# One written order of issue for the attention stage of a fused attention, Fourier-mix and gated-MLP kernel

## The chip, the cores and the metric

The kernel runs on one core of a Trainium2 chip. The metric is the device time of one execution in microseconds, lower is better. The engines are TensorE (PE, matmuls; PEld is its weight load), VectorE (DVE), ScalarE (ACT), GpSimd (POOL) and SyncE (SP, which issues DMAs).

## The reference, cut to what matters

```python
def reference(**kwargs):
    attn_out = _attn_ref(q, k, v, f)      # 4 batches x 8 heads, 576 tokens, 64 channels a head
    x = attn_out.transpose(0, 2, 1, 3).reshape(B, S, H * D)
    x = _moe_ref(x, w_ch1, w_ch2)         # real part of a 2-D FFT + x, norm, relu MLP 512-2048-512
    return _moe2_ref(x, w_theta, w_tok_r, w_tok_i, w_ch)

def _attn_ref(q, k, v, f):
    scores = scale * np.matmul(q, k.transpose(0, 1, 3, 2))
    cum = np.cumsum(np.log(np.clip(f, 0.0001, 1.0)), axis=-1)
    scores = np.where(causal, -1e9, scores + cum[:, :, :, None] - cum[:, :, None, :])
    attn = softmax(scores)
    return np.matmul(attn, v)
```

The change touches the issue order of the first stage alone: attention, and the FFTs of the batches that are already done.

## The kernel before

The program has three phases. `phase1` walks over the 32 heads in pairs (two heads, g = 0 and g = 1, share one 128-row result) and does the FFT of three batches and the first normalisation between the heads; `phase2` is the MLP (`ffn1`, `ffn2`); `phase3` is the token mix and the gate.

For one head, attention does this. `prep_units`: ACT rounds the raw q and k into `hi` (L222) and copies q (L224), POOL forms the rest (`hi` L226, `kl` L228). `score_units`: five tiles of query rows, i = 4 down to 0, with 576, 448, 320, 192 and 66 key columns; each is a matmul on `hi` (L247) and one on `kl` (L248) into a PSUM bank `pa` (three banks); DVE adds the mask and keeps the row minimum (L256), ACT takes the exponential into `P` (L261). `turn_units`: 15 PE transposes of `P` (L286) into four `pb` banks (three physical ones), each copied to `PT` by DVE or, the fourth, by ACT (L289). `av_units`: for a pair of heads, 14 matmuls of `v` (64 columns wide) with `PT` into the one bank `pt` (L321). Head g = 0 writes partitions 0 to 63 and head g = 1 writes 64 to 127, so the two heads' matmuls use different halves of the array. `spread` transposes the reciprocal row sums (`wide`, L300), `evac_pair` multiplies `pt` by them (L347, into `X` or `Y`), and `fft_units` has some 87 matmuls a batch (L428, L439, L451).

In the program text the 14 matmuls alternate between the heads: for each key block and column range `for g in (1, 0)` issues both. A dependency added by hand (the loop over `copies`, with reason "one run") lets the first of the 14 go only after all eight `PT` copies of the two heads are placed.

What order the engines see is not the text's. The Tile framework's scheduler reorders `phase1` by a timeline of its own and by priorities (`high_priority(20)` for scores, `high_priority(100)` for the 14 matmuls); the opening (heads 0 and 1's preparation and head 0's scores) and everything after the sixth column of the MLP are in `manual_schedule`, where program order is kept. PSUM slots are given out in the scheduler's order.

Of the kernel before, what the change touches and what calls it, by code (L numbers as in the profile page):

```python
# [17 lines left out]
B, H, S, D = 4, 8, 576, 64  # L18
# [35 lines left out]
G = 4  # L54


def f(ap):
    return ap.bitcast(F32)


class Net:
# [37 lines left out]
    def p1_open(self):  # L99
# [22 lines left out]
        )  # L122
        h0 = self.w3.tile([128, 1600], F32R, tag="PT", name="h0", bufs=4)[64:66]
        flag = f(h0[:, 2 * S : 2 * S + 1])
        self.P = [self.w3.tile([128, 1856], F32, name=f"P{k}", bufs=1) for k in range(2)]
        ch = self.c1.tile([32, 2, S], F32R, tag="E", name="ch", bufs=2)
# [14 lines left out]
        for z in self.q2:  # L141
            nc.gpsimd.memset(f(z[64:66]), 1.0)
# [5 lines left out]
        for z in (self.xh, self.xl):  # L148
            nc.gpsimd.memset(f(z), 0.0)
# [123 lines left out]
    def turn_units(self, hd):  # L273
        nc = self.nc
        P = hd["P"]
        PT = self.w3.tile([128, 1600], F32, tag="PT", name="PT", bufs=4)
        hd["PT"], hd["copies"] = PT, []
        for bank, pieces in enumerate(TURNED):
            ps = self.bank_b()
            for j, a, b, off in pieces:  # L280
                for i in range(5):
                    if not a <= TOP[i] < b:
                        continue
                    o, n = off + TOP[i] - a, END[i] - TOP[i]
                    src = P[0:n, POFF[i] + KEY[j] : POFF[i] + KEY[j] + 128]
                    nc.tensor.transpose(ps[:, o : o + n], src, self.ident[0:n, 0:n])  # L286
            d, w = TSKIP[bank], TWIDE[bank]
            dst = PT[:, PTOFF[bank] : PTOFF[bank] + w]
            copy = nc.scalar.copy(dst, ps[:, d : d + w]) if bank > 2 else nc.vector.tensor_copy(dst, ps[:, d : d + w])  # L289
            hd["copies"].append(copy)  # L290
            yield

    def spread(self, p, T, wide):
# [10 lines left out]
    def av_units(self, m, hds, T, wide, done):  # L304
        nc = self.nc
        v = hds[0]["pair"]["v"]
        place = {
            (j, max(a, 128 * j)): PTOFF[bank] + off - TSKIP[bank] + max(a, 128 * j) - a
            for bank, pieces in enumerate(TURNED)
            for j, a, b, off in pieces  # L310
        }
        yield
        first = True
        with self.tc.high_priority(100):
            for j in range(5):
                for lo_q, hi_q in ((0, SPLIT), (SPLIT, 576)):
                    a = max(lo_q, 128 * j)
                    if a >= hi_q:
                        continue
                    for g in (1, 0):  # L320
                        ins = nc.tensor.matmul(  # L321
                            T[64 * g : 64 * g + 64, T0 + a : T0 + hi_q],
                            v[:, j, g, :],
                            hds[g]["PT"][:, place[j, a] : place[j, a] + hi_q - a],
                            start=j == 0,
                            stop=j == 4 or (j == 1 and hi_q == SPLIT),
                        )
                        if first:
                            for copy in hds[0]["copies"] + hds[1]["copies"]:
                                self.tc.add_manual_dep(  # L330
                                    ins.ins, copy.ins.name,
                                    mybir.DependencyInfo(mybir.DependencyClass.NoSync, mybir.DependencyReason.DATA),
                                    reason="one run",
                                )
                            first = False
        for _ in range(5):
            yield
        R = self.spread(m % NP, T, wide)
        yield
        done(m, T, R)  # L340
# [137 lines left out]
    def phase1(self):  # L478
        pair, heads = self.p1_open()
        NH = B * H  # L480
        pairs, heads, raws = {0: pair}, dict(enumerate(heads)), {}
        fft = None
        self.tick = 0
        rows, norm, av = iter(()), iter(()), iter(())

        def pull():
            nonlocal fft
            next(rows, 0)
            self.tick += 1
            if self.tick % 3 == 0:  # L490
                next(norm, 0)
            if (self.tick % 5 or n > 24) and fft is not None and next(fft, 0) == 0:
                fft = None

        def done(m, T, R):
            nonlocal rows, fft
            for _ in rows:
                pass
            rows = self.evac_pair(m % NP, R, T, m == B * NP - 1)
            next(rows, 0)  # L500
            if m % NP == NP - 1:
                fft = self.fft_units(m // NP, *self.EO, rows)

        for n in range(-1, NH + 1):
            a = self.score_units(heads[n + 1], (n + 1) % 2) if 0 < n + 1 < NH else iter(())
            prep = iter(())
            if n + 2 < NH:
                p, g = divmod(n + 2, 2)
                if n == 0:
                    pairs[1] = self.load_pair(1)  # L510
                if n >= 0:
                    heads[n + 2] = dict(pair=pairs[p], g=n + 2)
                    prep = self.prep_units(n + 2, pairs[p], raws.pop(n + 2), heads[n + 2])
                if n > 0 and g == 1 and p + 1 < B * NP:
                    pairs[p + 1] = self.load_pair(p + 1)
            if n + 3 < NH:
                raws[n + 3] = self.load_head(n + 3)
            m, odd = divmod(n - 2, 2)
            if m >= 0 and not odd:
                T = self.bank_t()  # L520
                av = self.av_units(m, [heads[2 * m], heads[2 * m + 1]], T, pairs[m]["rz"], done)
            t = self.turn_units(heads[n]) if 0 <= n < NH else iter(())
            if n == NH - 1:
                self.p1a.close()
                self.p2_open()
                self.load(0)
                self.load(1)
            k = n - 2
            if 0 <= k < 4:
                for j in range(2):  # L530
                    self.load_dft(2 * k + j, f(heads[n]["hi"][0:1, 0, 0:2]))
            if n == NH - 3:
                while fft is not None:
                    pull()
                t1 = self.c1.tile([128, 2, CH], F32, tag="E", name="uc1", bufs=2)
                t2 = self.c1.tile([128, 2, CH], F32, tag="O", name="uc2", bufs=2)
                t3 = self.c1.tile([128, 2, CH], F32, tag="yh", name="s12", bufs=1)
                t4 = self.c1.tile([128, 2, CH], F32, tag="yl", name="sq", bufs=1)
                t5 = self.c1.tile([128, 4], F32, tag="zh", name="rs", bufs=1)
                norm = self.norm_units(0, ((t1, t2), t3[:, 0], t3[:, 1], t4, t5))  # L540
            live = True
            while live:
                live = False
                for g_ in (t, av, a):
                    if next(g_, 0) is None and (g_ is not av or n >= NH - 1):
                        live = True
                next(prep, 0)
                pull()
                if n >= NH - 1:
                    self.fill(2)  # L550
            for _ in prep:
                pass
        for _ in norm:
            pass
        self.p1b.close()
        for _ in rows:
            pass
        self.pt.close()
        self.pso = self.ctx.enter_context(self.tc.tile_pool(name="pso", bufs=2, space=PSUM))
        return fft  # L560
# [538 lines left out]
        self.pu0.close()  # L1099


def body(tc, ins, out):
    with ExitStack() as ctx:
        net = Net(ctx, tc, ins, out)
        fft = net.phase1()
        net.phase2(fft)
        net.phase3()
# [101 lines left out]
```

## Time and profile before

| | |
|---|---|
| median of 3 runs | 940.19 us (938.8 to 942.03) |
| profiled execution, own time | 940.95 us |
| its span | 939.2 us, 15860 instructions |
| busy over the span | PE 894.1 us (95%), PEld 841.5 us, DVE 606.7 us, ACT 417.8 us, POOL 326.3 us |
| mean granted PE clock | 0.985 |

Attention takes the first 245 us or so; head 31's transposes, the last batch's FFT and the first norms reach to about 305 us; from there the MLP and the token mix fill the rest. In the trace a matmul's record lasts beyond the start of the next (the engine is pipelined), so what PE needs for a matmul is read from the distance between two starts, not from a record's length.

### The profile page before, as it was taken

How to read it: one execution, taken by the hardware profiler on the slowest of the kernel's cores; microseconds unless marked ns; L12 is line 12 of the kernel's file. 1: busy time of each engine (PE TensorE's matmuls, PEld its weight loads, DVE VectorE, ACT ScalarE, POOL GpSimd, SP SyncE). 2: the span in 40 equal slices, each digit the busy share in tenths (PEclk: the TensorE clock that was granted, in tenths of full speed). 3: DMA queues.
4: the chain of work that ended last, by engine and by line, in shares of the span. 5: the costliest groups of instructions: out<-in, count | busy, mean ns of one | idle time of the engine just before them, and what ended most of it. 6: DMA issues, size and time to landing. Idle time of an engine off the chain costs nothing.

```text
span 939.2 us, 15860 instructions
## 1 busy us (share of the span) xinstructions
PE 894.1 (95%) x5960; PEld 841.5 (90%) x5960; DVE 606.7 (65%) x1495; ACT 417.8 (44%) x1014; POOL 326.3 (35%) x369
## 2 busy tenths in 40 slices
PE   4998999989788999999999999999999999999998
PEld 3777878777577999999999999999999999999998
DVE  8676676674899943456654565536687756747563
ACT  6888678685544332222221232223235534434331
POOL 6676788676601343000000000000035635425330
PEclk9999999999979999999999999999999999999999
DMA  5643423231233300013322122514310000010001
GB/s 167 202 149 106 130 93 114 83 105 40 82 97 93 90 1 1 1 46 90 91 91 90 45 90 74 199 29 127 109 51 2 1 26 27 14 40 1 26 27 51
DMA packets 23725, 68.04 MB, mean 72 GB/s; under 512 B 2906, under 2 KB 6362, under 8 KB 23648
## 3 DMA queue, kind: packets, MB, share of 16 engines
q1 hardware_dynamic: 20608, 62.88, 21.2%
q0 software_dynamic: 2320, 2.97, 1.2%
q10 hardware_dynamic: 720, 1.18, 0.4%
q8 instruction: 47, 0.77, 0.3%
q14 instruction: 30, 0.25, 0.1%
HBM read 57.91 MB, written 9.07 MB: 71 GB/s over the span
## 4 chain that ended last, share of the span: by engine, by line
PE 62%; DVE 5%; ACT 1%; issue 1%; DMA 0%; POOL 0%; DVEq 0%; SPq 0%; ACTq 0%
PE pa L767 19%; PE pb L781 11%; PE po L781 8%; PE pb L988 7%; PE pa L999 5%; PE pa L952 5%; PE po L988 5%; PE pa L948 1%; DVE u L789 1%; DVE kra L959 1%; DVE a L587 0%; DVE a L585 0%; DVE uc L754 0%; DVE kra L962 0%; PE pb L952 0%
## 5 line engine op out<-in xcount | busy, mean ns | idle before, releaser
L767 PE MATMUL pa<-un,wf 128*128 128x384 f32 x1152 | 221.4, 342 | 6.3 <-ACT un L755 3.4
L767 PEld LDWEIGHTS pa<-un,wf 128*128 128x128 f32 x1152 | 204.6, 191 | 10.2 <-DVE un L756 4.5
L773 DVE SCALAR_TENSOR_TENSOR h<-pa,h 128x384 fp32r<-128x384 f32 x96 | 52.4, 555 | 139.0 <-ACT h L772 139.0
L781 PE MATMUL pb<-h,wf 128*128 128x384 f32 x660 | 134.2, 337 | 0.3 <-DVE u L789 0.3
L781 PEld LDWEIGHTS pb<-h,wf 128*128 128x128 f32 x660 | 116.0, 188 | 1.1 <-DVE u L789 0.6
L781 PE MATMUL po<-h,wf 128*128 128x384 f32 x492 | 105.2, 340 | 0.4 <-ACT h L772 0.2
L772 ACT ACTIVATE h<-pa 128x384 fp32r<-128x384 f32 x96 | 45.7, 489 | 132.7 <-PE pa L767 130.0
L261 ACT ACTIVATE P<-P,mn 128x448 f32<-128x448 f32 (+4 forms) x160 | 89.0, 558 | 33.6 <-DVE mn L256 33.4
L988 PE MATMUL pb<-wtk,z 128*128 128x288 f32 x513 | 98.3, 295 | 1.3 <-ACT z L977 1.3
L944 POOL COPY xd<-u 128x64 f32<-128x64 f32 x32 | 6.9, 255 | 264.5 <-DVE u L789 254.5
L256 DVE CUSTOM_DVE_ANT_0 P<-pa,mask 128x448 f32<-128x448 f32 (+3 forms) x160 | 69.4, 457 | 42.1 <-PE pa L248 35.6
L781 PEld LDWEIGHTS po<-h,wf 128*128 128x128 f32 x492 | 86.2, 188 | 3.6 <-ACT h L772 1.9
L978 POOL TENSOR_TENSOR z<-kra,z 128x256 fp32r<-128x256 f32 x72 | 53.1, 752 | 93.5 <-ACT z L977 93.4
L247 PE MATMUL pa<-hi 128*128 128x448 f32 (+1 forms) x192 | 65.8, 364 | 20.5 <-DVE hi L226 9.4
L988 PEld LDWEIGHTS pb<-wtk,z 128*128 128x128 f32 x513 | 79.3, 188 | 2.0 <-ACT z L977 2.0
L988 PE MATMUL po<-wtk,z 128*128 128x288 f32 x351 | 75.2, 295 | 0.8 <-ACT z L977 0.8
L286 PE MATMUL pb<-ident,P 128*128 128x128 f32 (+2 forms) x480 | 73.9, 284 | 1.7 <-DVE uc L724 0.9
L247 PEld LDWEIGHTS pa<-hi 128*128 128x128 f32 x192 | 38.2, 204 | 30.1 <-issue 14.5
L289 DVE COPY PT<-pb 128x448 f32<-128x448 f32 (+1 forms) x96 | 55.6, 594 | 14.2 <-PE pb L286 13.3
L952 PE MATMUL pa<-wf,xs 128*128 128x256 f32 x456 | 64.1, 289 | 0.0
L286 PEld LDWEIGHTS pb<-ident,P 128*128 128x128 f32 (+2 forms) x480 | 56.6, 147 | 7.5 <-ACT P L261 1.2
L248 PE MATMUL pa<-kl,q 66*128 66x448 f32 (+1 forms) x192 | 58.0, 337 | 1.4 <-POOL kl L228 0.7
(206 smaller groups left out, 1667.0 us busy)
## 6 DMA issues: line engine op xcount, KB each, us to landing
raw<-in_qk SPq DMA_DIRECT2D x31, 576.0 KB
raw<-in_wf SPq DMA_DIRECT2D x32, 512.0 KB
raw<-in_wtk SPq DMA_DIRECT2D x18, 288.0 KB
v<-in_vp SPq DMA_DIRECT2D x16, 320.0 KB
out<-ob SPq DMA_DIRECT2D x12, 288.0 KB
dft<-in_dft POOLq DMA_DIRECT2D x8, 346.0 KB, 5.4
raw<-in_wth SPq DMA_DIRECT2D x4, 512.0 KB
st_wth<-raw SPq DMA_DIRECT2D x4, 512.0 KB
```

The costliest lines, as they stand in the source:

```text
L247: nc.tensor.matmul(t[:, 0 : b - a], hi[:, 1, q], hi[:, 0, a:b], start=True, stop=False)
L248: nc.tensor.matmul(t[:, 0 : b - a], q2[:, q], kl[:, g, a:b], start=False, stop=True)
L256: nc.vector.tensor_tensor_reduce(out=p[:, a:b], in0=t[:, 0 : b - a], in1=self.mask[:, m0 + a : m0 + b], scale=-0.125, scalar=least, op0=AL ...
L261: nc.scalar.activation(p, p, AF.Exp, bias=lowest, scale=-1.0, accum_out=zs[:, g, i : i + 1])
L286: nc.tensor.transpose(ps[:, o : o + n], src, self.ident[0:n, 0:n])
L289: copy = nc.scalar.copy(dst, ps[:, d : d + w]) if bank > 2 else nc.vector.tensor_copy(dst, ps[:, d : d + w])
L767: nc.tensor.matmul(ps[:, 0:CH], t[:, l, 128 * d : 128 * d + 128], un[r][:, d], start=n == 0, stop=n == 11)
L773: nc.vector.scalar_tensor_tensor(h[:, 1], ps[:, 0:CH], 0.0, f(h[:, 0]), ALU.max, ALU.subtract)
L781: nc.tensor.matmul(outs[d], t[:, l, 128 * d : 128 * d + 128], h[:, r], start=k % G == 0 and n == 0, stop=k % G == G - 1 and n == 2,)
L952: nc.tensor.matmul(th, xs[:, l, d], self.wth[d][:, r, 256 * hf : 256 * hf + 256], start=n == 0, stop=n == 11)
L978: nc.gpsimd.tensor_tensor(z[:, 1], t, f(z[:, 0]), ALU.subtract)
L988: nc.tensor.matmul(acc[k][th], z[:, l, 128 * k : 128 * k + 128], self.wtk[kt][:, r, 288 * th : 288 * th + 288], start=first and i == 0 and ...
```

## The change

All calls of `phase1` on engines and queues, from the start of its loop (head 0's transposes, head 1's scores) to the point where head 31's transposes are about to be created, go to a `Recorder` instead of the builder. Then `rec.emit(order(0, n))` issues the recorded calls inside `manual_schedule` for all engines, in one fixed permutation that is written out as a string: each character gives the distance of the next call in the list of those left. So each engine keeps its part of one order, and PSUM slots follow that order. The hand-made dependency on the `PT` copies is gone, so that each of the 14 `av` matmuls has a place of its own. Which instructions there are, and their sizes, does not change. The recording ends before the last head's transposes, the last `av` run, the last FFT and the MLP; these go through the scheduler as before.

```diff
+class Recorder:
+    def __getattr__(self, name):
+        return Queue(self, name)
+
+    def emit(self, order):
+        for k in order:
+            engine, name, a, kw = self.calls[k]
+            getattr(getattr(self.nc, engine), name)(*a, **kw)
+        self.live = False
...
-            copy = nc.scalar.copy(dst, ps[:, d : d + w]) if bank > 2 else nc.vector.tensor_copy(dst, ps[:, d : d + w])
-            hd["copies"].append(copy)
+            (nc.scalar.copy if bank > 2 else nc.vector.tensor_copy)(dst, ps[:, d : d + w])
...
-                        if first:
-                            for copy in hds[0]["copies"] + hds[1]["copies"]:
-                                self.tc.add_manual_dep(
...
-                                    reason="one run",
...
+        rec = self.nc = Recorder(self.nc)
...
             if n == NH - 1:
+                with self.tc.manual_schedule():
+                    rec.emit(order(0, len(rec.calls)))
+                self.nc = rec.nc
                 self.p1a.close()
...
+DIGITS = "#$%&()*+,-./0123456789:;<=>?@ABCDEFGHIJKLMNOPQRSTUVWXYZ[]^_`abcdefghijklmnopqrstuvwxyz|"
+ORDERS = (
+    (
+        "&~$6~+X~,e~,e~,e~,e#*35=)129*+1(%((-%.*..vw#$+##///~$-#.$,(#&))#~$%$6#((<^>/#u,8B$.U%....2.~*p2#~*n5"
...
+def order(part, n):
+    left, taken, digits = list(range(n)), [], iter(ORDERS[part])
+    for c in digits:
+        k = DIGITS.find(c)
...
+        taken.append(left.pop(k))
+    return taken
```

In the rows below `pt` is the result bank of a pair of heads, `PT` the transposed probabilities (one number for each head), `P0` and `P1` the probabilities of the even and the odd head; all recorded calls carry line 71 in the changed kernel.

PE in the first pair of heads, before: the first 14 matmuls of the pair come in two runs, the heads in turn.

```order
L321 MATMUL pt_342<-PT_281,v_119 64x192
L321 MATMUL pt_342<-PT_212,v_119 64x192
L321 MATMUL pt_342<-PT_281,v_119 64x384
L321 MATMUL pt_342<-PT_212,v_119 64x384
L321 MATMUL pt_342<-PT_281,v_119 64x64
L321 MATMUL pt_342<-PT_212,v_119 64x64
L321 MATMUL pt_342<-PT_281,v_119 64x384
L321 MATMUL pt_342<-PT_212,v_119 64x384
L247 MATMUL pa_400<-hi_298 128x320
L248 MATMUL pa_400<-kl_205,q21_100 128x320
```

PE at the same pair in the changed kernel: head 0's matmuls (`PT_207`) stand one by one between head 1's scores and transposes, before head 1 has any `PT`.

```order
L71 MATMUL pb_217<-ident_68,P0_107 128x128 x3
L71 MATMUL pt_238<-PT_207,v_119 64x384
L71 MATMUL pa_216<-hi_161 128x320
L71 MATMUL pa_216<-kl_110,q21_100 128x320
L71 MATMUL pa_218<-hi_161 128x192
L71 MATMUL pa_218<-kl_110,q21_100 128x192
L71 MATMUL pt_238<-PT_207,v_119 64x384
L71 MATMUL pb_225<-ident_68,P1_108 128x128
L71 MATMUL pa_219<-hi_161 128x66
L71 MATMUL pa_219<-kl_110,q21_100 128x66
L71 MATMUL pb_230<-ident_68,P1_108 128x128 x2
L71 MATMUL pt_238<-PT_207,v_119 64x320
```

What moved: the alternation of the two heads is broken up, and other work stands between.

PE in the middle of the changed kernel (a later pair, `pt_605`): four matmuls of one head, then five of the other with a score between, and only the end alternates.

```order
L71 MATMUL pt_605<-PT_561,v_498 64x384
L71 MATMUL pt_605<-PT_585,v_498 64x384
L71 MATMUL pa_603<-hi_566 128x66
L71 MATMUL pa_603<-kl_538,q20_99 128x66
L71 MATMUL pt_605<-PT_585,v_498 64x384
L71 MATMUL pt_605<-PT_585,v_498 64x192
L71 MATMUL pt_605<-PT_585,v_498 64x64
L71 MATMUL pt_605<-PT_585,v_498 64x320
L71 MATMUL pt_605<-PT_561,v_498 64x320
L71 MATMUL pt_605<-PT_585,v_498 64x192
L71 MATMUL pt_605<-PT_561,v_498 64x192
```

Before, this pair too came in alternating runs of 8 and 6 or of 14.

PE at the end of the recorded part, in the changed kernel: head 31's last score tiles stand right in front of its transposes (`P1_108`).

```order
L71 MATMUL pa_848<-hi_826 128x192
L71 MATMUL pa_848<-kl_756,q21_100 128x192
L71 MATMUL pa_849<-hi_826 128x66
L71 MATMUL pa_849<-kl_756,q21_100 128x66
L326 MATMUL pa_3177<-ident_68,wide_806 128x128
L313 MATMUL pb_3169<-ident_68,P1_108 128x126
L313 MATMUL pb_3169<-ident_68,P1_108 128x128 x3
```

Before, 12 transposes of head 30 (`P0_107`) stood between them:

```order
L248 MATMUL pa_3152<-kl_2698,q21_100 128x66
L286 MATMUL pb_3104<-ident_68,P0_107 128x128 x4
L300 MATMUL pa_3174<-ident_68,wide_2936 128x128
L286 MATMUL pb_3129<-ident_68,P0_107 128x128 x2
L286 MATMUL pb_3129<-ident_68,P0_107 128x66
L286 MATMUL pb_3129<-ident_68,P0_107 128x126
L286 MATMUL pb_3140<-ident_68,P0_107 128x128 x3
L286 MATMUL pb_3166<-ident_68,P1_108 128x126
```

What moved there: head 30's transposes went ahead of head 31's last scores.

Counted over PE's whole order: the 224 `av` matmuls stand in 25 runs before and in 63 after. Before, all form 112 neighbouring pairs of one width and two heads. After, 49 such pairs are left (15 of 64 columns, 12 of 320, 12 of 384, 10 of 192), 28 pairs have two widths (the wider one is 384 in 18 of them, 192 in 8, 320 in 2), and 70 matmuls have no partner (26 of 192, 22 of 384, 17 of 64, 5 of 320).

From the second column of the MLP to the end each engine's order is the same in both.

## Rows read from the trace of the kernel before

**Rows 1.** Busy time by stage, instructions in brackets (windows of the whole core).
```profile
core 0: us, PE busy (x) PEld busy (x) DVE busy (x) ACT busy (x) POOL busy (x), PEclk, DMA share, GB/s
0.00:25.00 25.00, 12.05 (x41) 9.74 (x41) 21.42 (x44) 16.02 (x33) 14.15 (x37) 1.00 0.60 183
25.00:100.00 75.00, 70.44 (x527) 56.04 (x528) 52.24 (x192) 65.28 (x189) 54.47 (x48) 1.00 0.48 148
100.00:245.00 145.00, 133.87 (x1033) 111.21 (x1033) 96.02 (x336) 100.99 (x286) 107.14 (x101) 0.98 0.27 85
245.00:305.00 60.00, 49.63 (x298) 42.39 (x298) 56.74 (x118) 29.27 (x59) 11.52 (x13) 0.87 0.35 106
305.00:940.00 635.00, 628.11 (x4067) 622.11 (x4066) 380.24 (x808) 206.26 (x450) 139.00 (x172) 1.00 0.17 53
```

**Rows 2.** PE's waits, 25 to 245 us: total us, times, longest.
```profile
PE pa L247 <- POOL hi L226: 3.5, 2, 2.6
PE pa L247 <- DVE mn L256: 3.4, 9, 0.8
PE pt L321 <- DVE PT L289: 2.8, 4, 1.3
```

**Rows 3.** PE in order of time: start, length, what.
```profile
120.17 0.39 PE L247 MATMUL pa<-hi 128*128 128x320 f32 x1
120.40 0.31 PE L248 MATMUL pa<-kl,q 66*128 66x320 f32 x1
120.55 0.25 PE L247 MATMUL pa<-hi 128*128 128x192 f32 x1
...
120.75 0.60 PE L286 MATMUL pb<-ident,P 128*128 128x128 f32 x4
121.11 0.28 PE L247 MATMUL pa<-hi 128*128 128x66 f32 x1
...
122.05 0.48 PE L451 MATMUL pb<-dft,yh 128*128 128x290 f32 x2
...
123.31 0.43 PE L248 MATMUL pa<-kl,q 66*128 66x448 f32 x2
```

**Rows 4.** PE in order of time around two runs of the 64-wide matmuls.
```profile
125.62 1.95 PE L321 MATMUL pt<-PT,v 128*64 128x192 f32 x16
127.50 0.66 PE L286 MATMUL pb<-ident,P 126*128 126x126 f32 x4
...
128.15 0.31 PE L248 MATMUL pa<-kl,q 66*128 66x320 f32 x1
128.39 1.20 PE L321 MATMUL pt<-PT,v 128*64 128x320 f32 x12
```

**Rows 5.** PE in order of time at a full-width f32 matmul (two records), and the last run.
```profile
241.95 0.83 PE L722 MATMUL pb<-s,mean 128*128 128x384 f32 x2
242.62 0.60 PE L286 MATMUL pb<-ident,P 126*128 126x126 f32 x4
...
249.42 2.93 PE L321 MATMUL pt<-PT,v 128*64 128x192 f32 x28 [0.36 <-DVE PT L289]
```

**Rows 6.** PE groups by form, 25 to 245 us: busy, mean ns, idle before.
```profile
L286 PE MATMUL pb<-ident,P 128*128 128x128 f32 x357 | 59.3, 283 | 1.1 <-DVE uc L724 0.9
L321 PE MATMUL pt<-PT,v 128*64 128x384 f32 x120 | 25.0, 509 | 0.0
L286 PE MATMUL pb<-ident,P 126*128 126x126 f32 x59 | 16.9, 287 | 0.4 <-DVE yl L430 0.4
L247 PE MATMUL pa<-hi 128*128 128x320 f32 x30 | 11.0, 368 | 0.2 <-DVE mn L256 0.2
```

**Rows 7.** DVE and ACT groups by form, 25 to 245 us.
```profile
L256 DVE CUSTOM_DVE_ANT_0 P<-pa,mask 128x320 f32<-128x320 f32 x30 | 14.5, 484 | 9.3 <-PE pa L248 9.3
L256 DVE CUSTOM_DVE_ANT_0 P<-pa,mask 128x66 f32<-128x66 f32 x29 | 6.4, 220 | 2.2 <-PE pa L248 2.2
L261 ACT ACTIVATE P<-P,mn 128x320 f32<-128x320 f32 x30 | 16.7, 556 | 7.9 <-DVE mn L256 7.9
L261 ACT ACTIVATE P<-P,mn 128x66 f32<-128x66 f32 x30 | 10.3, 345 | 0.7 <-DVE mn L256 0.7
```

More of the change, by code (lines that the diff above doesn't have):

```diff
@@ L58, in f, with __init__, __getattr__, call @@
     return ap.bitcast(F32)
+class Recorder:
+    def __init__(self, nc):
+        self.nc, self.calls, self.live = nc, [], True
+    def __getattr__(self, name):
[5 more added lines that the diff above has]
+        self.live = False
+class Queue:
+    def __init__(self, rec, engine):
+        self.rec, self.engine = rec, engine
+    def __getattr__(self, name):
+        def call(*a, **kw):
+            if not self.rec.live:
+                return getattr(getattr(self.rec.nc, self.engine), name)(*a, **kw)
+            self.rec.calls.append((self.engine, name, a, kw))
+        return call
 class Net:
@@ L276, in turn_units @@
         PT = self.w3.tile([128, 1600], F32, tag="PT", name="PT", bufs=4)
-        hd["PT"], hd["copies"] = PT, []
+        hd["PT"] = PT
         for bank, pieces in enumerate(TURNED):
@@ L312, in av_units @@
         yield
-        first = True
         with self.tc.high_priority(100):
@@ L320, in av_units @@
                     for g in (1, 0):
-                        ins = nc.tensor.matmul(
+                        nc.tensor.matmul(
                             T[64 * g : 64 * g + 64, T0 + a : T0 + hi_q],
@@ L327, in av_units @@
                         )
-                        if first:
-                            for copy in hds[0]["copies"] + hds[1]["copies"]:
-                                self.tc.add_manual_dep(
-                                    ins.ins, copy.ins.name,
-                                    mybir.DependencyInfo(mybir.DependencyClass.NoSync, mybir.DependencyReason.DATA),
-                                    reason="one run",
-                                )
-                            first = False
         for _ in range(5):
@@ L1099, in phase3 @@
         self.pu0.close()
+DIGITS = "#$%&()*+,-./0123456789:;<=>?@ABCDEFGHIJKLMNOPQRSTUVWXYZ[]^_`abcdefghijklmnopqrstuvwxyz|"
+ORDERS = (
+    (
+        "&~$6~+X~,e~,e~,e~,e#*35=)129*+1(%((-%.*..vw#$+##///~$-#.$,(#&))#~$%$6#((<^>/#u,8B$.U%....2.~*p2#~*n5"
+        "14-[#*.,#11+#&*+*-1133#J%%***H&B)#%+.$68%8&,$+)/***(++,,)**$1)))$(#&FG)#P%&&&&K(+$#%((()$(**&888.7$#"
+        "3=.-=$2#$0-*...2-33#,*-3.2G5G#4D(1#*7)6-P<P#%//)#-%IG,G(&$++B%?($==(-%-$-*12202)/&/.)$4(+$&)$J(J,(%#"
+        "%#O#/%%%#$%%(E$&#%&&))#560/44$$2+/#0$/*..-1-1+/#.3/2#5(4#4*(1*1#0%66#QR%*/*.(-$I$&HH*,&+2(%:<&<0(%/,"
+        "5625$(++)--*-$,)$*)%/(.(%&&%#$M&$%%%H&&)%($&&(($))45%4-%20$0%0#0*.--1+,/#..0+,.,)0012+14#33-33#&**IJ"
+        "#-&F%FF*&++B&%/&7/%&+#&+*.*.()++,)++*$)2)$($-&&$%#$#L/%#$$$%E%$&#%%&&#((3/3$2$1/+#.$..---1-+/#..3/-1"
+        ")445)5,4Y#(X/)#,,000#0)%.J%(I*H*,(+&1;=(=1)&#,),1,$+0+)-F..*-,$+4+$%0)%(((%#%$&&$%%&++&L%*$))**$%<=="
+        "&<&9(;(8$A1&67>>5?#03$2:205$;.:$.9/78$#6+<<.7$$5.4+X3W)*U%U,T$00+5HJ(J,<&,:E$D/A7A%@66&55559(+%+1)&*"
+        "/./5/(..$1$0+//555/4446645:###21#&3#2(1111#0&$%#((3$22%M#0$/((-/8(.B..,--%,~)*+/+#7$6..#533,--(,*-+#"
+        "6&5#E&&C))((#&,/#....%-/+.+--%>>0*//$.*$,,,(+**&*&))--0*/).+-(&++$*&))%,)*()1**0()))..,--%-&,<,&+*&7"
+        ")))))))9))))#(O*()L))*#=)(*&))$))%**45&4.&20%0&00///#2.,0$//1,-/-*112#2+14#333(#*0+//#.)&%+,,,-&,..R"
+        "+Q&%.&(,,)%*%))((%&&**3#&%&%&-&~&Q&&%++)$))*$8))$((&$%0%%%%%%%=#$&&$%%%%%$N##A#%%#G$$%%#&&&#&~$R&~$Q"
+        "~%i)%(11#~%c,<00~%_0$/70%///3#.1;66--+-29#833#<,;6(1#9.8.#)%L%L%LM#4&*&))2B&9$`/(/)...&1-1A1%11,0%$."
+        "($*%=3*)))&%&&&#%9($E7&$%%&&H%($&&(($9#99$8$5&7&4#>.%222#181.#44)-4-3+#&.99#3*2,1166677#&O(3N$(MNK)+"
+        "1)0G*&C,BB%,@@&?2%/1689%8-$4$41*06605555%446$%($&*,&$---+$,,#)--#,,&+$*#+++$U++*$2&1%0&#.&&,$+7+%*@,"
+        ",#+++~(y+.)//.*3)2#(00++#*,*(#,+++#*%)#(((%2$14((%.&&.---%,,,%$113,,$++.)--.(-(88$^&]D)+&M***())-)))"
+        "$%+Z+&**%)(((%&&(L(&&R&(/(((&----.&-$T,%++&)%(((((($&&#%L(%&I&&((&#($&&(($))34%3-%1/$/%/#.---1-+/#.."
+        "0/-.)112)22k#(j-)#**...#.&%,...&-),)++&%))**1&91)%&/,#(1+&$)-&(+**%)&((%&((~%y$&&%~%u&$6%$$$$10$$9$$"
+        "$$$$##((%J#%%&&O%(#&&&$%%F#$$##%%#$%%($&#..+-:3~$4#~$3~%12$~%/,,,0,--/#..,8-2+,0)#66*0#....211#0&&/%"
+        ".JK(,H#6(1&++;=&?=$K7;;&(,---%,1,=1%0$*($*%*2)=))&%&&&#%+(*(%(Q$&D(M(&,$++,,%//;<*;5*97$$6+665559#42"
+        "6&5572)53/)60555#(4.366677#+4s.s$+p#p,o;):+k%,--5#==I``&_$^*&))))((333(%11(0&22;2G2&&&%%%)%*D+(....%"
+        "--/#%%$)$))$()/))$(#$%#&#%%%%4%#$$&&$%%&&#$&&&&#%%(#&$%&&)%$&&#%#$$$###$$++#l**#)(((((,#+q&*#Sl)%((("
+        "#M&&)))$((((((,,,,$+++++7777F79D&JJ&7$***()$0&(((&&**:&))&//(.&-000&002/#)%:K#(I&/&.E(>&1(1##/$$--+2"
+        "2$1).0$////$,&$++%**#@)$((&&%(($&$%&&)%(($((++##$$#%######"
+    ),
+)
@@ L1102, in body @@
+def order(part, n):
+    left, taken, digits = list(range(n)), [], iter(ORDERS[part])
+    for c in digits:
+        k = DIGITS.find(c)
+        if k < 0:
+            k = DIGITS.index(next(digits)) * len(DIGITS) + DIGITS.index(next(digits))
+        taken.append(left.pop(k))
+    return taken
 def body(tc, ins, out):
```

## The prediction

> **What bounds the kernel now.** I read the busy time by stage first, then PE's waits, then PE in order of time. From 305 us on PE is busy 628.1 of 635 us [rows 1], and each engine's order there is the same before and after, so that stretch can only move as a block. What can change is the attention, 0 to 245 us, and the 60 us behind it. In 25 to 245 us PE shows 70.44 + 133.87 = 204.3 busy of 220 us, ACT 166, POOL 162, DVE 148 [rows 1]. By this PE is nearly full, 15.7 us are idle, and the named waits are small ones: 3.5 us for POOL, 3.4 us for a score bank that DVE still reads, 2.8 us for a `PT` copy [rows 2].
>
> The record lengths hide more. A transpose is recorded with 283 ns [rows 6], but three of 128 columns and one of 66 start 0.36 us apart in all (120.75 to 121.11), some 0.105 us for a full one [rows 3]. So I price what PE needs by distances of starts. Scores: `hi` and `kl` of 320 and 192 columns take 0.58 us (120.17 to 120.75) [rows 3], 0.57 ns a column; a head has 3,204 columns and a short tile of 66 that takes 0.22, some 1.95 us; the 30 heads of the stretch [rows 6] make 59 us. Transposes of `P` and `wide`: 473 full ones (357 + 59 [rows 6] and 57 of `wide`) and 43 short ones, 52 us. FFT: 9 matmuls of 290 columns in 1.26 us (122.05 to 123.31) [rows 3], 261 in the stretch, half of them of 258 columns or fewer, 34 us. The 64-wide matmuls, 15 pairs of heads (120 records of 384 columns, 8 a pair [rows 6]), at the price worked out below, 46 us. Sum 191 us. So some 29 us of the 220 are waits, 15.7 in sight and the rest under the modelled ends. I take 30, since the prices are rounded up. That is all that a better order can return here.
>
> A way to read this from one row is PEld, the weight load: 56.04 + 111.21 = 167 of 220 us, which would leave 53 us [rows 1]. The Trainium skill (Perfetto Trace Analysis, Identifying the Most-Contended Engine) says just this: judge TensorE's headroom by the busy share of the weight loads, not of the matmuls. By that figure the sum below would gain up to 23 us more. The starts in order of time bear out that there is more headroom than the 15.7 us, but not the 53: the 64-wide f32 matmuls stream longer than their weights load.
>
> **What the change costs.** No instruction is added. But PE pays for the place of the 64-wide matmuls. Two of them that follow each other for the two heads run side by side: eight pairs of records, 1,024 columns a head, end 1.88 us after their start (125.62 to 127.50) [rows 4]. One f32 matmul over the full width takes 0.67 us for its two records of 384 columns (241.95 to 242.62) [rows 5], 1.74 ns a column. At this price 1,024 columns take 1.78 us, so the two heads together cost what one does, and a matmul without its partner costs the whole price again. In units of columns that PE streams: before 16 x 1,600 = 25,600. After, from the counts that stand with the change: 49 equal pairs 11,328 (15 x 64 + 12 x 320 + 12 x 384 + 10 x 192), 28 unequal pairs by the wider 9,088 (18 x 384 + 8 x 192 + 2 x 320), 70 alone 16,128 (26 x 192 + 22 x 384 + 17 x 64 + 5 x 320); together 36,544. The 10,944 more make 19.0 us. A partner that ends early lets the next one start in some unequal pairs: I take 18. Bounds: 13 if each unequal pair overlaps fully with its neighbours, 19 if none does.
>
> Then the way in and out. Behind a run the next matmul starts 1.88 - 1.78 = 0.10 us late, and before one the 320-column `kl` takes 0.24 (128.15 to 128.39) [rows 4] in place of 0.15 (120.40 to 120.55) [rows 3]: 0.09 us. So 0.19 us a run, and 38 runs more (63 for 25) make 7.2 us. The Trainium skill (TensorEngine Tiling (Array Packing), Key Properties) speaks against the change here: a switch of the tiling mode drains TensorE. The trace agrees with 0.19 us a visit; without that rule the sum would be 7 us better.
>
> PE's need thus rises by 25 us. Not all lies on the path. In the first 25 us PE issues 41 matmuls [rows 1] and mostly waits for heads 0 and 1 to arrive. The first two pairs carry 2,430 of the extra columns and 11 of the extra runs, 6.3 us, and their first matmuls now stand in front of head 1's short tiles, where PE had nothing ready. I take 5 of the 6.3 as free; bounds 0 and 6.3. On the path: 20 us.
>
> **What it returns.** The waits for other engines. PE's order gets longer against the unchanged work of POOL, DVE and ACT, so these run ahead of PE by more with each pair, and the waits for POOL and for `PT` copies should die out after the first heads. What stays are the loops that start on PE itself. Score to transpose for the 320-column tile: 0.484 (DVE) + 0.556 (ACT) [rows 7] and some 0.3 for hand-overs, 1.4 us; for the 66-column tile 0.220 + 0.345 [rows 7] and the same, 0.9. Between a tile's last score matmul and its first transpose the new order has more PE work than this in 156 of 160 cases, and between the last use of a PSUM bank and its next in 379 of 390 (before: 368). So few waits are built in. I take 5 us for what stays of the 30: 25 returned. Bounds: 0 returned (the waits move but stay), and 30.
>
> At the end head 31's transposes follow its last scores with nothing between, where 12 transposes (1.2 us) of head 30 stood: the chain of the 66-column tile, 0.9 us, is now open, +1. What is late next is the stretch to 305 us, where DVE is busy 56.7 of 60 us [rows 1] and starts when its last attention work is done; it holds the same work and moves as a block with the attention's end.
>
> **Sum.** +18 + 7 - 5 - 25 + 1 = -4 us on the profiled execution's 940.95 us, which is 0.8 us above the median of the runs: 937 us. All edits of the text (recorder, dropped dependency) cost nothing at run time: they leave the instruction list as it is. SP's transfers are in the one order too; each raw head is loaded into a buffer that POOL and ACT free, and these get earlier against PE.
>
> **Rivals.**
> *Slower: the split matmuls cost more than the waits return.* One mechanism: the 63 visits and the lost pairs are certain, read from order and rows, while the waits only may go. If more than some 9 of the 30 us stay, the change loses. With half of them (15) it is 20 + 1 - 15 = +6, 947; with all of them +21, 962. For it: the new order cuts transposes into single pieces, each with a wait of its own for ACT. Against it: the covers counted above. Chance 30%.
> *No change that can be measured.* The two sides are of one size (20 to 25 us each), so that they cancel within 0.3% (2.8 us, about what a measurement of this kernel can tell from no change) if 6 to 12 us of waits stay: 938 to 943. Chance 24%.
> *Clearly faster, 920 to 930.* The order was made for the first heads' latency too, all 30 us go and a few more at the start, where PE's first 25 us hold 13 us of idle time [rows 1]: 20 + 1 - 30 - 4 = -13, 928. The headroom of the weight loads would allow still more. Chance 12%.
> *The forecast, 930 to 938:* 34%.
>
> The likeliest is 937 with its own range 930 to 943. The range 924 to 954 leaves out the case in which nearly nothing is returned and the far end of the clearly faster one. Faster by over 0.3%: 0.46 (forecast and clearly faster); within it: 0.24; slower: 0.30.
>
> **What would show it.** In the changed profile: (1) lone 64-wide matmuls of 384 columns that hold PE 0.67 us each; in all 36,544 x 1.74 ns = 64 us under these matmuls at most, where 25,600 columns made 45. (2) PE's idle time in the attention under 8 us, no wait for POOL over 1 us after the fifth head. (3) The start of the last `av` run some 4 us earlier than its 249.42 us [rows 5]. (4) From 305 us on the same 635 us. Wrong it would be if the unpaired matmuls overlap with other work after all (then the gain is nearer 20 us), or if DVE or ACT, whose order is now fixed, hold PE up at every tile: then DVE's waits for PE and PE's for `mn` grow together.

## The result and the profile after

The changed kernel takes 948.07 us (947.08 to 949.56, 4 runs) where the kernel before took 939.76 beside it: ratio 1.0086, interval 1.0061 to 1.0111. It is slower by about 8 us; 937 and "faster" were forecast. The rival that came true is *slower*, in its number (947 with half of the waits left); of its reason, waits that stay, the trace shows little.

The windows of the changed kernel, the stretches of [rows 1] (columns as there):

```profile
core 0: us, PE busy (x) PEld busy (x) DVE busy (x) ACT busy (x) POOL busy (x), PEclk, DMA share, GB/s
0.00:25.00 25.00, 12.50 (x40) 8.99 (x40) 21.83 (x39) 15.02 (x31) 14.25 (x37) 1.00 0.60 181
25.00:100.00 75.00, 74.63 (x484) 52.40 (x483) 48.33 (x182) 61.05 (x171) 48.12 (x42) 1.00 0.44 135
100.00:245.00 145.00, 144.11 (x1056) 116.84 (x1057) 99.24 (x342) 106.10 (x297) 112.05 (x106) 1.00 0.29 92
245.00:305.00 60.00, 52.29 (x315) 45.42 (x312) 54.27 (x117) 28.74 (x63) 12.90 (x14) 0.86 0.32 97
305.00:940.00 635.00, 629.01 (x4060) 622.74 (x4060) 384.42 (x815) 208.94 (x455) 139.45 (x172) 0.99 0.16 53
```

PE is now busy 218.7 of the 220 us from 25 to 245, against 204.3 in [rows 1], and yet has passed fewer instructions (484 + 1056 for 527 + 1033). The list of PE's waits in that stretch is down to two lines (total us, times, longest), where [rows 2] had POOL, `mn` and `PT`:

```profile
PE pb L71 <- DVE ea L71: 0.4, 1, 0.4
PE pb L71 <- DVE oa L71: 0.3, 1, 0.3
```

So the order did what was forecast of the waits, and the kernel is slower all the same: PE is full, with more to do. What fills it shows in PE's order of time (start, length, what):

```profile
143.75 0.66 PE L71 MATMUL pb<-ident,P 128*128 128x128 f32 x4
144.34 0.86 PE L71 MATMUL pt<-PT,v 128*64 128x384 f32 x2
145.13 0.33 PE L71 MATMUL pb<-ident,P 128*128 128x128 f32 x1
```

One 64-wide matmul of 384 columns (two records) without its partner holds PE from 144.34 to 145.13, 0.79 us with its way out.

The table sums the distances from each PE start to the next, less the idle time that the profile prints, from the first score at 9.4 us to the start of the last one. A *couple* is two 64-wide matmuls of the two heads, of one width and one right behind the other; a *run* of 64-wide matmuls is one visit, with a way in (a longer step before it) and a way out (a late start behind it). The last run comes after the last score and is not in the table. Two of the experiments below stand beside the two kernels.

| us | before | after | couples together | before's order, heads apart |
|---|---|---|---|---|
| start of the last score | 243.1 | 247.8 | 234.5 | 262.8 |
| 64-wide matmuls with the way out (runs) | 46.1 (24) | 68.4 (62) | 49.7 (46) | 72.7 (24) |
| scores | 75.6 | 72.2 | 74.6 | 74.0 |
| transposes of `P` and `wide` | 58.2 | 57.4 | 58.2 | 56.0 |
| FFT | 35.7 | 36.1 | 36.1 | 36.1 |
| PE idle in sight | 17.4 | 3.7 | 5.7 | 13.9 |
| inside the rows of work: lost at half pace in the opening | 10.1 | 6.7 | 7.8 | 7.5 |
| inside the rows of work: lost at a granted clock of 0.50 later | 3.4 | 0 | 0 | 0 |

The 64-wide matmuls cost 22.3 us more, and 38 more ways in, 0.09 each, lie in the rows of the work ahead of them: 3.4. Of these 25.7 us the attention lost 4.8, so some 21 came back. Not all of it is waits. The last two lines are estimates, half of the time in which PE worked at half pace.

The kernel before twice ran at a granted clock of 0.50 (1.2 of 2.4 GHz) for 3.41 us, from 145.75 and from 210.60 us, and lost 1.7 us each time, the second time in a run of 64-wide matmuls; the changed kernel has 1.00 there. The windows of the kernel before:

```profile
140.00:150.00 10.00, 8.69 (x60) 8.14 (x56) 6.76 (x26) 8.32 (x25) 9.08 (x10) 0.83 0.26 93
210.00:220.00 10.00, 9.22 (x55) 6.20 (x56) 2.72 (x16) 5.45 (x15) 9.77 (x9) 0.83 0.30 93
```

And in the opening PE's starts lie about twice as far apart as later (before: ten transposes from 18.64 to 20.74 us, 0.21 each for 0.105), up to 33.1 us in the kernel before and 25.9 in the changed one. The 1.00 that [rows 1] prints there says nothing of it: the trace has no clock row before these points. The order alone does not set this end. The run *cover at the tail* below has the changed kernel's order up to the tail, and its half pace lasts until 31.4 us. The same matmul in the changed kernel, then there:

```profile
26.86 0.75 PE L71 MATMUL pt<-PT,v 128*64 128x320 f32 x2
27.54 0.44 PE L71 MATMUL pb<-ident,P 128*128 128x128 f32 x2
```

```profile
27.60 1.33 PE L71 MATMUL pt<-PT,v 128*64 128x320 f32 x2
28.86 0.69 PE L71 MATMUL pb<-ident,P 128*128 128x128 f32 x2
```

It holds PE for 0.68 and for 1.26 us, and the second pair's last matmul starts at 50.46 and 52.91 us.

So the 21 us are 13.7 of idle time (17.4 less 3.7), 3.4 of the half clock and 3.4 of an opening that was shorter in this profile. With both taken out, the 64-wide rows go from 44.4 to 67.2 us, and scores, transposes and FFT from 157.7 to 160.2: 25.3 more to do, and nothing hidden in those rows came back.

At the tail, PE in order of time, changed kernel:

```profile
254.24 4.62 PE L346 MATMUL pt<-PT,v 128*64 128x192 f32 x28
258.78 0.94 PE L768 MATMUL pb<-ident,rs 128*128 128x128 f32 x6
262.14 0.44 PE L788 MATMUL pa<-un,wf 128*128 128x384 f32 x1 [2.42 <-ACT un L776]
```

The last run starts 4.8 us later than in [rows 5] and takes 4.62 us in place of 2.93, 3.41 us of it at a granted clock of 0.50. The span is 6.1 us longer (945.3 for 939.2): 4.8 is lost by the last run, 1.3 behind it.

### The profile page after: what moved, and what is told of

Its sections match the earlier page's. It is cut to its first block, busy times and chain, and to the rows that moved or that the text cites. A ratio compares the mean times of both kernels' runs of the same rounds, so it can differ in the third digit from the quotient of the medians.

```text
span 945.3 us, 15839 instructions
## 1 busy us (share of the span) xinstructions
PE 914.6 (97%) x5960; PEld 848.2 (90%) x5960; DVE 609.0 (64%) x1495; ACT 419.9 (44%) x1014; POOL 326.8 (35%) x369
## 4 chain that ended last, share of the span: by engine, by line
PE 86%; DVE 8%; POOL 2%; ACT 1%; issue 1%; DMA 0%; DVEq 0%; ACTq 0%; POOLq 0%
PE pa L788 20%; PE pb L802 12%; PE po L802 9%; PE pb L71 9%; PE pt L71 7%; PE pb L1009 6%; PE pa L71 6%; PE pa L1020 5%; PE pa L973 4%; PE po L1009 4%; DVE kra L980 1%; DVE kra L983 1%; PE pa L969 1%; PE pb L468 1%; POOL u L71 1%
## 5 line engine op out<-in xcount | busy, mean ns | idle before, releaser
L71 ACT ACTIVATE P<-P,mn 128x576 f32<-128x576 f32 (+4 forms) x155 | 86.5, 560 | 25.9 <-DVE mn L71 25.4
L71 DVE CUSTOM_DVE_ANT_0 P<-pa,mask 128x448 f32<-128x448 f32 (+3 forms) x155 | 67.4, 457 | 44.3 <-PE pa L71 41.7
L71 PE MATMUL pb<-ident,P 128*128 128x128 f32 (+2 forms) x465 | 82.7, 281 | 2.2 <-DVE PT L71 1.6
L71 PE MATMUL pt<-PT,v 128*64 128x192 f32 (+3 forms) x420 | 72.7, 372 | 0.3
L1009 PEld LDWEIGHTS po<-wtk,z 128*128 128x128 f32 x351 | 57.3, 188 | 1.2 <-ACT z L998 1.2
```

The costliest lines, as they stand in the source:

```text
L71: getattr(getattr(self.nc, engine), name)(*a, **kw)
L1009: nc.tensor.matmul(acc[k][th], z[:, l, 128 * k : 128 * k + 128], self.wtk[kt][:, r, 288 * th : 288 * th + 288], start=first and i == 0 and ...
```

## The experiments

Theory 1: the loss is the price of lost couples and visits on a PE that is full. Theory 2: the waits are only covered by PE's longer work, and return when it is shortened. Theory 3: the loss lies at the tail.

**Couples together.** In the changed kernel, each couple is joined at the later one's place:

```diff
-                    rec.emit(order(0, len(rec.calls)))
+                    rec.emit(couples(order(0, len(rec.calls)), self.av))
+def couples(taken, av):
+    for calls in av.values():
+        for b, a in zip(calls[0::2], calls[1::2]):
+            i, j = sorted((taken.index(b), taken.index(a)))
+            taken.insert(j - 1, taken.pop(i))
+    return taken
```

> The changed kernel with one edit: of each g = 1 and g = 0 couple of 64-wide matmuls, the earlier one is moved right in front of the later one's place; the rest of the order is kept. All 112 couples are side by side again, runs fall from 63 to 47. Theory 1 (the loss is what PE needs: 17 us of lost pairs, 0.19 us a run): 17 + 16 x 0.19 = 20 us less than the changed kernel's 948, some 928 (925 to 933), so 11 below the kernel before. Theory 2 (PE's longer order only covered waits, and these come back when PE gets shorter): 938 to 945, with PE waits of 10 us or more in 25 to 245 us. Theory 3 (the loss lies at the tail, in the clock and in head 31's open chain): 945 or more.

Measured: 931.84 us, ratio to before 0.9911 (0.9897 to 0.9926), 16 us below the changed kernel and the fastest kernel here. PE in order of time, with a couple of 384 columns for each head:

```profile
135.36 0.87 PE L71 MATMUL pt<-PT,v 128*64 128x384 f32 x4
136.16 0.33 PE L71 MATMUL pb<-ident,P 128*128 128x128 f32 x1
```

Two matmuls (four records) take 0.80 us, as long as the lone one's 0.79. That is the price of a lost couple in two rows: the whole matmul. The windows show PE still nearly full, at a granted clock of 1.00:

```profile
25.00:100.00 75.00, 73.57 (x534) 54.67 (x533) 51.10 (x186) 63.37 (x182) 54.96 (x47) 1.00 0.47 144
100.00:245.00 145.00, 140.75 (x1093) 114.34 (x1092) 104.50 (x360) 110.79 (x308) 111.72 (x109) 1.00 0.28 94
```

Theory 1 holds in the main. The 64-wide rows fall by 18.7 us, and the last score starts 13.4 earlier. Theory 2 has a small part: 2.0 us of idle time are back. The rest stands in the rows of scores (2.4) and transposes (0.8), of which some 2.3 us is the opening, at half pace until 28.5 us here.

**One run a pair.** All 14 matmuls at the place of the last:

```diff
+def one_run(taken, av):
+    for calls in av.values():
+        last = max(calls, key=taken.index)
+        rest = [k for k in taken if k not in calls]
+        at = taken.index(last) - len(calls) + 1
+        taken = rest[:at] + calls + rest[at:]
+    return taken
```

> The changed kernel with all 14 of a pair's 64-wide matmuls put in one run, the heads in turn, at the place of the last of the 14; the rest of the order is kept. Runs fall from 63 to 16. Theory 1 (pairs and visits price the order, and little else waits): 17 + 47 x 0.19 = 26 us less than 948, some 922 (918 to 928), and 6 below the kernel with the couples alone. Theory 2 (waits come back): 936 to 945. Theory 3 (tail): 945 or more. Between: a run of 14 stands late, so the PT buffers and the result bank come free later; if that shows, PT copies or transposes wait and it is slower than the couples alone.

Measured: 955.89 us, ratio 1.0162 (1.0148 to 1.0176). By its number this fits the tail's case alone (945 or more), and not by its reason, since the last score already starts 9.7 us later than in the changed kernel. The windows:

```profile
25.00:100.00 75.00, 67.10 (x457) 50.43 (x455) 45.25 (x167) 56.18 (x164) 46.24 (x40) 0.91 0.42 135
100.00:245.00 145.00, 137.55 (x1019) 112.74 (x1019) 91.53 (x324) 103.72 (x290) 103.96 (x95) 0.94 0.28 91
```

PE is idle for 15 us and its clock is below 1.00. Where from, PE in order of time:

```profile
99.13 0.55 PE L71 MATMUL pb<-ident,P 128*128 128x128 f32 x3
100.86 0.30 PE L71 MATMUL pa<-hi 128*128 128x66 f32 x1 [1.19 <-DVE mn L71]
...
102.18 0.44 PE L71 MATMUL pb<-ident,P 128*128 128x128 f32 x2 [0.16 <-ACT P L71]
103.08 0.58 PE L71 MATMUL pb<-dft,el 128*128 128x258 f32 x1 [0.46 <-POOL el L71]
...
105.81 4.69 PE L71 MATMUL pt<-PT,v 128*64 128x192 f32 x28
110.44 0.47 PE L71 MATMUL pa<-hi 128*128 128x448 f32 x1
```

and the granted clock of the same stretch:

```profile
100.00:102.00 2.00, 1.14 (x7) 0.85 (x7) 2.00 (x9) 2.00 (x6) 0.39 (x1) 1.00 0.00 0
102.00:104.00 2.00, 1.38 (x7) 1.12 (x7) 0.11 (x2) 2.00 (x5) 1.92 (x2) 0.65 0.00 0
104.00:106.00 2.00, 2.00 (x11) 1.64 (x12) 0.81 (x2) 1.97 (x8) 1.92 (x3) 0.50 0.00 0
106.00:108.00 2.00, 2.00 (x12) 1.03 (x13) 0.73 (x2) 0.06 (x1) 2.00 (x3) 0.50 0.00 0
```

The 64-wide matmuls had stood between a score and the transposes that need its row minimum and exponential. With them gone PE waits for `mn` (a score whose bank DVE still reads) and `P` (a transpose whose exponential ACT still forms), the granted clock then falls to 0.50, and the record of the run lasts 4.69 us for 2.93 in [rows 5]. Against the couples alone, at the last score: idle 17.9 for 5.7, +12.2; granted clock 0.50, half of PE's working time in these stretches, +14.9 (estimate); with that taken out, the 64-wide rows 42.6 for 49.7, -7.1 with 31 visits fewer, and the transposes 59.1 for 55.7, +3.4, for a reason that was not settled; sum +23.4, measured +23.0.

**Before, heads apart.** In the kernel before, the loop over the heads is put outside:

```diff
-            for j in range(5):
-                for lo_q, hi_q in ((0, SPLIT), (SPLIT, 576)):
...
-                    for g in (1, 0):
+            for g in (1, 0):
+                for j in range(5):
+                    for lo_q, hi_q in ((0, SPLIT), (SPLIT, 576)):
```

> The kernel before with the loops of the 14 matmuls turned round: the 7 of one head, then the 7 of the other, in the same runs and behind the same copies. No couple is left but the one at the seam. If a matmul without its partner holds PE for its own columns (1.74 ns each, 25,600 columns more), PE needs 42 to 44 us more; the waits of the kernel before (25 us by theory 1) absorb part of it: 955 to 965. If two matmuls run side by side whatever stands between them in one run, or the price of a lost pair is smaller than the rows say: within 5 us of 940.

Measured: 971.12 us, ratio 1.0324 (1.0308 to 1.034), above the 955 to 965 expected. A run of 14 now reads

```profile
60.38 5.25 PE L321 MATMUL pt<-PT,v 128*64 128x192 f32 x28
```

against 2.93 in [rows 5]. The 64-wide matmuls take 79.0 us for 46.1. But the scheduler moved other work too, and nearly all of the 33 us arrived at the end, so for the waits this run is not clean; the last pair of experiments mends that.

**Cover at the tail.** Head 30's last transposes go behind head 31's last scores again:

```diff
+            if mark is not None and bank >= 2 and hd["g"] == B * H - 2:
+                self.late += range(mark, len(nc.calls))
...
+                    rec.emit(put_late(order(0, len(rec.calls)), self.late))
```

> The changed kernel with the last two groups of head 30's transposes (and their copies) moved behind head 31's last scores, as the kernel before had them, so that head 31's last chain from score to transpose is covered. The part after the recorded stretch is planned anew and differs a little. By the price of the prediction (+1 us for the open chain): 1 to 2 us less than 948. If the tail is where most of the loss lies (last run 254.24 us against 249.42, its length 4.62 us against 2.93 at a lower clock): 4 to 6 us less.

Measured: 949.29 us, ratio 1.0094 (1.008 to 1.0108): no gain. The last run is short again,

```profile
256.34 2.93 PE L350 MATMUL pt<-PT,v 128*64 128x192 f32 x28
```

and it does not help. In the profile this kernel is 2.5 us late from the opening on (above); the last run's end is only 0.4 late, so some 2 us are won up to there, with the run at a granted clock of 1.00. But the first MLP matmul then waits longer for ACT (3.33 us for 2.42),

```profile
263.46 0.65 PE L792 MATMUL pa<-un,wf 128*128 128x384 f32 x1 [3.33 <-ACT un L780]
```

and the span ends 2.7 us later than the changed kernel's. Theory 3 falls.

**Fewer and more visits.** On top of the couples, a run moves back to the pair's next run if at most 4, or 8, PE instructions stand between (31 and 20 runs); or, the other way, later couples are pushed behind one or more PE instructions that follow (60 runs):

```diff
+        for one, two in zip(runs, runs[1:]):
+            if tensor(taken, calls, one[-1], two[0]) <= most:
+                taken = [k for k in taken if k not in one]
+                at = taken.index(two[0])
+                taken[at:at] = one
```

> The changed kernel with its couples together, and, further, each run of a pair's 64-wide matmuls moved back to the pair's next run where at most 4 other PE instructions stand between. Runs fall from 47 to 31, all couples stay. If a visit costs 0.19 us and the cover that is taken from score and transpose is not missed: 16 x 0.19 = 3 us less than the couples alone (931.8), some 929. If waits come back in its place: 932 or more, with PE's idle time before its last score above 6 us.

> The same with at most 8 other PE instructions between: 20 runs. By the price of visits alone 27 x 0.19 = 5 us less than the couples alone, some 927. As one run a pair (16 runs) brought 12 us of idle time and stretches at half clock and took 956, I expect part of that here: above the kernel with at most 4 between, 930 to 945; a granted clock below 1.00 in 25 to 245 us would show the same cause.

> The changed kernel with its couples together, and runs of several couples taken apart by pushing the later couples behind one, two or more of the PE instructions that follow: 60 runs for 47, all couples stay side by side, cover is hardly touched. By 0.19 us a visit: 13 x 0.19 = 2.5 us more than the couples alone (931.8), some 934.3. If a visit costs nothing once PE is busy: 932.

Measured: 933.48 (ratio 0.9918, 0.9902 to 0.9933), 957.41 (1.0165, 1.0144 to 1.0187) and 940.31 us (0.9993, 0.9985 to 1.0002). With 31 runs the couples' gain is kept but nothing added: idle time before the last score is 11.1 us for 5.7, with `mn` back among PE's waits:

```profile
PE pa L71 <- DVE mn L71: 3.9, 5, 1.1
```

With 20 runs it is the one-run case again: idle 15.6, granted clock 0.90 and 0.94 in the same two windows.

With 60 runs the price of a visit can be read from one stretch. The kernel with the couples alone, then the one with 60 runs:

```profile
137.36 1.31 PE L71 MATMUL pt<-PT,v 128*64 128x192 f32 x12
138.60 0.55 PE L71 MATMUL pb<-ident,P 128*128 128x128 f32 x3
139.08 1.20 PE L71 MATMUL pt<-PT,v 128*64 128x320 f32 x12
140.21 0.47 PE L71 MATMUL pa<-hi 128*128 128x448 f32 x1
```

```profile
139.09 0.55 PE L71 MATMUL pt<-PT,v 128*64 128x192 f32 x4
139.56 0.33 PE L71 MATMUL pb<-ident,P 128*128 128x128 f32 x1
139.82 0.34 PE L71 MATMUL pt<-PT,v 128*64 128x64 f32 x4
140.09 0.33 PE L71 MATMUL pb<-ident,P 128*128 128x128 f32 x1
140.34 0.87 PE L71 MATMUL pt<-PT,v 128*64 128x384 f32 x4
141.14 0.33 PE L71 MATMUL pb<-ident,P 126*128 126x126 f32 x1
141.40 1.20 PE L71 MATMUL pt<-PT,v 128*64 128x320 f32 x12
142.53 0.47 PE L71 MATMUL pa<-hi 128*128 128x448 f32 x1
```

The same work takes 2.85 us with two runs and 3.44 with four: 0.30 us a visit. Over the whole attention, with the time at half pace taken out, the 64-wide rows of the six kernels whose couples are whole are 42.6, 43.2, 44.4, 45.6, 49.7 and 51.7 us (16, 20, 25, 31, 47 and 60 runs): 0.21 us a run for the way out (estimate), with 0.09 for the way in 0.30 again. By the last score the kernel with 60 runs is 4.6 us behind the couples alone, 0.35 a visit (0.5 of the 4.6 is the opening); the rest of its 8 us is lost behind the attention.

**Before's order in the table, and the same with heads apart.** The permutation string is replaced by the one in which the scheduler had placed the same calls: each engine then has the order of before, instruction for instruction. The second kernel changes nothing but the order inside each run:

```diff
+        for run in runs:
+            places = sorted(taken.index(k) for k in run)
+            one = [k for k in run if mine.index(k) % 2 == 0]
+            for at, k in zip(places, one + [k for k in run if k not in one]):
+                taken[at] = k
```

> The changed kernel with another permutation in its table: the one in which the scheduler placed the same calls in the kernel before, so that every engine has the order of before while the calls are recorded and issued in one written order, banks too. If the form of the change costs nothing and only the permutation does: 940, within 0.3% of the kernel before. If handing out banks in the order of issue or the lost dependency costs by itself: 943 or more.

> The same permutation of before, but in each run of the 64-wide matmuls first those of one head and then those of the other, in the same places: no couples, nothing else moves. In the kernel before with turned loops the time under these matmuls rose from 46.1 to 79.0 us, but there the scheduler had planned anew. If a longer PE lets the other engines run ahead so that waits die out (the prediction's reason for 25 us returned): 33 us more of PE, of which 15 to 20 come back, 953 to 958, and PE idle before its last score falls from 17.4 us to under 5. If the waits are set by the order (chains that start on PE itself and lack cover): 966 to 974 with 12 us or more still idle.

Measured: 939.99 us (ratio 0.9989, 0.9979 to 0.9999) and 960.5 (1.0216, 1.0196 to 1.0237). So recording, banks in order of issue and the dropped dependency cost nothing; only the permutation counts. The second lies between the two cases expected; its idle time to the last score, 13.9 us, is that of the second (12 or more). Its 64-wide matmuls take 26.6 us more, and the last score starts 19.7 later (20.4 against the kernel with before's order in the table). But PE's idle time fell by only 3.5 us (2.6 against that kernel); the rest lies in the two lines on half pace (7.5 us in all, for 10.1 + 3.4). PE's waits there, 25 to 245 us:

```profile
PE pa L71 <- DVE mn L71: 3.3, 9, 0.8
PE pt L71 <- DVE PT L71: 2.7, 4, 1.2
PE pa L71 <- DMA kl<-ch: 0.9, 1, 0.9
```

Beside [rows 2] POOL's `hi` is gone, and the waits for `mn` and `PT` are nearly as they were. A longer PE let POOL run ahead here; it did nothing for the waits that start on PE itself.

## Why the prediction went wrong

The step that failed is the fund of waits: "some 29 us of the 220 are waits ... I take 30", and from it "25 returned". About 14 us of waits returned. What PE needs was forecast well in sum, and its parts were shifted.

- *PE's need, +25.* Measured 25.3 to 25.7. 38 visits at 0.30 are some 11 us (7 forecast at 0.19), which leaves some 14 for the lost couples (18 forecast, bounds 13 and 19). That the sum came out is in part luck. The Trainium skill (TensorEngine Tiling (Array Packing), Key Properties) says that a change of tiling mode drains TensorE; the price of visits agrees with that in kind, and the runs give it its size.
- *5 of 6.3 us free in the first two pairs.* The number fits: the last matmul of the second pair starts at 50.5 us for 49.9, 0.6 later, 1.3 forecast. The reason does not: 3.4 us of it is the opening at half pace, which ended 7 us earlier in this one profile. In the profile of *cover at the tail*, with the same order, that matmul starts 3.0 us later than before. So some 2 to 3 of the 6.3 were free.
- *25 returned.* From 25 to 245 us PE's idle time fell from 15.7 to 1.3 us: 14 returned, nearly all that was in sight. The half clock of the kernel before, 3.4 us, went with the waits; the forecast had no term for it. In pairs 3 to 6 nothing came back on balance: the lag rose from 0.6 to 8.8 us, for some 6 of cost (1.5 a pair: 25.7 less 6.3, over 13 pairs); PE had been idle for only 4.6 us from 25 to 100 [rows 1]. In the nine pairs to 241 us, with some 13 of cost, it fell to 4.7, so that some 17 returned, the half clock among it.
- *Why the fund was too large.* It was a remainder: 220 less the sum of the shortest distances between starts, 191. In the kernel before, the 29 us were some 15 of idle time in sight, 7 of half pace (estimate: 3.8 in the opening behind 25 us, 3.4 at a granted clock of 0.50) and 6 to 7 of prices that were too low: at full pace scores take 63.2 us for 59, transposes 53.6 for 52 and FFT 35.7 for 34. Waits hidden under the modelled ends, for which the forecast took some 13, were not found: in the changed kernel, where PE is idle 1.3 us, scores, FFT and transposes still take more than those prices, 63.5 us for 29.5 heads' scores, 2.15 a head and not 1.95, and 36.1 for 261 FFT records and not 34. The reading by the weight loads (the Trainium skill, Perfetto Trace Analysis, Identifying the Most-Contended Engine) would have misled further: they are busy for 52.40 + 116.84 = 169.2 of 220 us while PE has no time left.
- *Why the waits went.* The forecast's reason, other engines running ahead of a longer PE, explains the smaller part: in before's order, with 26.6 us more under the 64-wide matmuls, idle time to the last score fell by 3.5 us, the size of POOL's wait. The rest is the permutation: with the couples together, and 5.3 us more under the 64-wide matmuls (49.7 for 44.4), it fell by 11.8. In the changed kernel it fell by 13.7. Each figure rests on one profiled execution.
- *The tail, +1, and "a block" behind it.* Cover there is worth nothing that shows at the end. The stretch of 245 to 305 us is not quite a block: 1.3 us were lost in it here, 3.5 in the kernel with 60 runs against the one with the couples, none between that one and before (8.6 us ahead at the last run, 8.8 at the end). Its granted clock is 0.86 to 0.91 in all of them; which wait there decides was not settled.

Of the signs that the forecast named, lone matmuls and PE's idle time came out as it said (0.79 us with the way out; 3.7 us idle, no POOL wait), and the last run's start did not: 254.24 us, 4.8 late and not 4 early. The 64-wide rows, ways out included, came to 68.4 us to the last score and the last run behind it, over the 64 that it named for the matmuls.

The sum with the measured terms: 25.3 of need, less 13.7 of waits, 3.4 of half clock and 3.4 of the opening, makes +4.8 at the end of the attention (forecast -4 with the tail), with 1.3 behind it +6 on the profiled span. The medians say +8. The changed kernel's four runs lie at 947.1 (two, one of them profiled) and at 949.1 and 949.6, about the 2.5 us apart that the opening made between two profiles of its order; that the opening is the reason was not shown.

The change thus holds a good half and a bad half. The order of scores, transposes and copies returns some 12 us of waits and 3.4 of half clock; taking 63 couples apart costs some 14, and 38 more visits some 11. Keeping the order and joining the couples gives 931.84 us, 0.9% below the kernel before.

## What to carry to other kernels

When the busiest engine gets more work in exchange for fewer waits, put the sure price against the idle time that the trace prints, stretch by stretch, and not against a remainder from best-case prices. Look in such a remainder for stretches at half pace, too: they are neither waits nor work. Matmuls that share the array in couples should stay next to each other in the engine's order: here one alone took as long as both. And separate waits that a longer engine absorbs (another engine that lags) from those that begin on that engine itself (score, minimum, exponential, transpose): here cover in between removed the second kind, and a longer PE did not.

## What the chip showed beside this

Short waits of PE can cost twice. In the kernel before, one 2.58 us wait was followed by a granted clock of 0.50 from 210.60 to 214.01 us, and the run behind it took 4.59 us for the 2.93 of [rows 5] (PE in order of time):

```profile
207.35 0.28 PE L248 MATMUL pa<-kl,q 66*128 66x66 f32 x1
210.21 0.47 PE L247 MATMUL pa<-hi 128*128 128x448 f32 x1 [2.58 <-POOL hi L226]
210.60 4.59 PE L321 MATMUL pt<-PT,v 128*64 128x192 f32 x28
```

With one run a pair, three waits of 0.2 to 1.2 us between 99 and 104 us were followed by the same, and over the attention the clock cost more than the added idle time (14.9 us by the estimate above, for 12.2). It does not always come: with 31 runs PE was idle for 11.1 us, in waits of up to 1.1, and the granted clock stayed at 1.00. The prediction had priced every wait by its length alone.
